# Issuing the row gather of a routed block one block earlier, at the end of the block before

## The chip, the cores and the metric

The kernel runs on one core of a Trainium2 chip. The metric is the device time of one execution in microseconds (us), from several runs; a profile of one more execution shows what each engine did. The engines are PE (TensorE: matmuls and transposes; its weight loads are listed as PEld), DVE (VectorE), ACT (ScalarE), POOL (GpSimd) and SP (SyncE, which here only issues DMAs).

## The reference

Three independent results make the output: a chunked attention, a mixture of four experts over 2304 tokens, and a routed mixture of eight experts, the last of which the change touches. Its core is:

```
expert_idx = np.argmax(logits, axis=1)
gate_w = probs[np.arange(N), expert_idx]
out = np.zeros((N, D), dtype=np.float32)
for e in range(E):
    mask = expert_idx == e
    xe = x[mask]
    h = np.maximum(xe @ w1[e], 0.0)
    ye = h @ w2[e]
    out[mask] = gate_w[mask, None] * ye
```

N is 2304, D 512, the inner size F 1024, E 8. Each token goes through the two weight matrices of one expert only, so the tokens of an expert must be collected (gathered), worked on together, and their results put back (scattered) to where the tokens stand.

## The kernel before, in words

Attention and the first mixture come first. During them the routing of the second mixture is worked out, and a table in DRAM, `slots`, lists which token stands in which slot and with which gate weight. The rows of the tokens lie in DRAM as `ytok`. The last part of the program (from about 785 us to the end at 1102) works through this table in **blocks** of at most 256 slots, one expert to a block.

`step` runs one block as 8 chunks of 128 inner columns. A chunk multiplies the block's rows, transposed (`x`), by a piece of the first weights (ps_h: lines L483 to L485 for a full block, a PAIR; L500 and L501 for a block of 192 rows, a MID), lets ACT and DVE make the activation out of ps_h (L488 and L489, or L506, L507, L511, L514), and later multiplies it by a piece of the second weights (ps_o, L543). Full precision is kept by splitting numbers into a high and a low part (L430 on ACT, L431 on DVE). `single` runs a block of 128 rows in plain fp32 matmuls (L1340 first, L1332 second).

Around the chunks of a block stand:

- `fetch_slots`: SP loads the slots of the block after the next one into `slot_then` (L939).
- `gather_y`: POOL casts the token numbers of the next block to integers (`src`, L942), and issues two indirect DMAs that gather 128 rows of 2 KB each from ytok into yb0 and yb1 (L944).
- `prep`: in the block's last chunk PE transposes the gathered rows (L955, eight transposes for 256 rows), and ACT and DVE write `x` for the next block (L961, L962).
- `finish_parts`: in the first chunk of the block after, ACT scales the results into an `ot` buffer (L983; L975 first adds the parts of a smaller piece), and POOL scatters them to the output by an indirect DMA (L984). The row numbers for it, `dst`, are written by DVE in the fourth chunk (L1353 in `single`, L1422 in `step`), once the scatter that reads the old ones has landed.

The slots move on through three buffers, `slot_then` to `slot_next` to `slot_now`, by two DVE copies in the first chunk of each block (L1394 and L1396).

How many blocks of each kind are needed depends on the routing, so most blocks stand under nested conditions `tc.If(counts > u)` that each engine tests by itself (L1451 for the PAIR blocks, L1462 and L1464 for a MID with a `single` behind it, L1473 and L1475 for further MIDs). In this run these are executed: the blocks 0 to 3 (unconditional), one PAIR, three times a MID and a `single`, one MID, and the last PAIR. Where the rest of a nest is skipped, each engine adds to its semaphores what the skipped blocks would have added; POOL does it for the counters of its DMAs. These places are called joins below. They are at about 939 us (J1, L1451), 1046 us (J2, L1464) and 1067 us (J3, L1475).

Each engine executes its instructions in the order in which this code issues them.

Of the kernel before, what the change touches and what calls it, by code (L numbers as in the profile page):

```python
# [24 lines left out]
KF = FF // P  # L25
# [9 lines left out]
NFIRST = 3  # L35
# [30 lines left out]
def attn_moe_moe2(ctx, tc, att, probs, wg, wgt, w12, m2w, out):  # L66
    nc = tc.nc
# [16 lines left out]
    def ps(tag):  # L84
        return ring(psum, "ps_" + tag, {"h": 2, "o": 4, "m": 2}[tag], [P, 512], F32)
# [51 lines left out]
    slots = dram.tile([NSLOT, 2], F32, name="slots")  # L137
# [173 lines left out]
    def x_sums(which=slice(0, 4)):  # L311

        b11, b21 = xraw[:, 0, 0:2, :], xraw[:, 0, 2:4, :]
        b12, b22 = xraw[:, 1, 0:2, :], xraw[:, 1, 2:4, :]
        t1, t2, t4 = [xsum[:, i] for i in range(3)]
        for out, a, b in ((t1, b12, b11), (t2, b22, t1), (b12, b22, b12), (t4, b21, t2))[which]:
            nc.gpsimd.tensor_tensor(out=out, in0=a, in1=b, op=ALU.subtract)

    def x_split(g):
        raw = (xraw[:, 0, 0:2, :], xsum[:, 0], xsum[:, 1], xraw[:, 1, 2:4, :], xraw[:, 1, 0:2, :],  # L320
               xraw[:, 0, 2:4, :], xsum[:, 2])[len(xs[g])]
        xh, xl = x_slot()
        nc.scalar.copy(xh, raw)
        nc.vector.tensor_tensor(out=xl, in0=raw, in1=xh.bitcast(F32), op=ALU.subtract)
        xs[g].append((xh, xl))
# [120 lines left out]
    def split_lows():  # L446

        while lows:
            lows.pop(0)()
# [248 lines left out]
    buf = {}  # L698
# [237 lines left out]
    def fetch_slots(c, to):  # L936
        assert c in ready or c < NFIRST
        row = nc.sync.value_load(start32[0:1, c:c + 1], min_val=0, max_val=NSLOT - BLK)
        nc.sync.dma_start(out=buf[to], in_=slots[bass.ds(row, BLK), :].rearrange("(i p) c -> p i c", p=P))  # L939

    def gather_y():
        nc.gpsimd.tensor_copy(buf["src"], buf["next"][:, :, 1])  # L942
        for i in range(2):
            nc.gpsimd.indirect_dma_start(  # L944
                out=buf["y"][i], out_offset=None, in_=ytok,
                in_offset=bass.IndirectOffsetOnAxis(ap=buf["src"][:, i:i + 1], axis=0),
                bounds_check=NT - 1, oob_is_err=False,
            )

    def prep(one=False):  # L950

        for i in range(1 if one else 2):
            tp = ps("m")
            for k in range(KD):
                nc.tensor.transpose(tp[:, k * P:(k + 1) * P], buf["y"][i][:, k * P:(k + 1) * P], ident)  # L955
            tpv = tp.rearrange("p (k x) -> p k x", x=P)
            xh, xl = [buf["x"][:, :, q, i * P:(i + 1) * P] for q in range(2)]
            if one:
                nc.scalar.copy(buf["xone"], tpv)
                continue  # L960
            nc.scalar.copy(xh, tpv)  # L961
            nc.vector.tensor_tensor(out=xl, in0=tpv, in1=xh.bitcast(F32), op=ALU.subtract)  # L962
# [92 lines left out]
    for g in range(1, len(GROUPS)):  # L1055
        pcs = att_pieces(g)
        if g == 1:
            then = [x_sums] + [lambda g=g: x_split(g)] * 7
        else:
            then = [lambda k=k: x_sums(slice(k, k + 1)) for k in range(4)] + [lambda g=g: x_split(g)] * 2  # L1060
# [211 lines left out]
    for i in range(NPLAIN):  # L1272
        e, fc = divmod(i, KF)
# [38 lines left out]
    def hold(banks, sizes):  # L1312
        held.append((banks, sizes))
# [5 lines left out]
    def single(s, c):  # L1319

        first = NM1 + s * KF
        assert [stream[q] - first for q in ("load", "split", "freed")] == [KF, 0, 0], (s, stream)
        stream["at"] = s, c
        stream["split"] = first + KF
        stream["limit"] = first + 2 * KF
        x = buf["xone"]
        o = rings["ps_o"][1][2]
        parts = {}

        def second(fc):  # L1330
            raw, h = parts.pop(fc)
            nc.tensor.matmul(o, lhsT=h, rhs=raw[-1][:, -D:], start=(fc == 0), stop=(fc == KF - 1))  # L1332

        for fc in range(KF):
            stream["call"] += 1
            raw, _ = raws.pop(first + fc)
            raw = raw if isinstance(raw, tuple) else (raw,)
            hp = ps("h")
            for k in range(KD):
                nc.tensor.matmul(  # L1340
                    hp[:, :P], lhsT=raw[0][:, k * P:(k + 1) * P], rhs=x[:, k, :], start=(k == 0), stop=(k == KD - 1)
                )
            h = buf["one"][fc]
            nc.scalar.activation(h, hp[:, :P], AF.Relu)
            parts[fc] = (raw, h)
            if fc == 0:
                nc.vector.tensor_copy(buf["now"], buf["next"])
                nc.vector.tensor_copy(buf["next"], buf["then"])
                gather_y()
            for _ in range(2 if 2 * fc < len(buf["raw_one"]) else 0):  # L1350
                load_next()
            if fc == 3:
                nc.vector.tensor_tensor(out=buf["dst"], in0=buf["now"][:, :, 1], in1=over[:, c, :], op=ALU.add)  # L1353
                fetch_slots(c + 2, "then")
            if fc >= LAGONE:
                second(fc - LAGONE)
            if fc == KF - 1:
                prep()
            if fc >= KF - NSPLIT:
                split_next()  # L1360
                split_lows()
        for fc in range(KF - LAGONE, KF):
            second(fc)
        hold([o], ONE)
        stream["freed"] = first + KF
        ahead = [stream[q] - first - KF for q in ("load", "split", "freed")]
        assert ahead == [KF, NSPLIT, 0] and not lows, (s, ahead)

    def step(s, c, sizes, one=False):

        ends = [finish_parts(*h) for h in held]
        held.clear()
        for end in ends:
            next(end, None)
        banks = []
        rings["ps_o"][0] = 0
        x = buf["x"]
        if sizes == PAIR:
            x = (lambda k: buf["x"][:, k, 0]), (lambda k: buf["x"][:, k, 1])
        more = s < NSTEP - 1  # L1380

        second = s == NFIRST - 1
        stream["at"] = s, c
        stream["stop"] = NM1 + (s + 1) * KF if one else NCHUNK
        if s >= NFIRST:
            stream["limit"] = NM1 + (s + 1) * KF
        for fc in range(KF):
            chunk(NM1 + s * KF + fc, x, sizes, fc, banks, True, finish if one else hold,
                  [lambda: prep(one)] if fc == KF - 1 and more else [])
            if fc == 0:  # L1390
                for end in ends:
                    for _ in end:
                        pass
                nc.vector.tensor_copy(buf["now"], buf["next"])  # L1394
                if more and not second:
                    nc.vector.tensor_copy(buf["next"], buf["then"])  # L1396
                    gather_y()
            if s <= NFIRST:
                if s + fc == 0:
                    flush(1)  # L1400
                    sides.append(last_routing())
                else:
                    side()
            if fc == 0 and more:
                ahead = s + 2 < NFIRST or s >= NFIRST
                if s < NFIRST:
                    stream["limit"] = NM1 + (s + (3 if s + 2 < NFIRST else 2)) * KF
                if second:
                    fetch_slots(c + 1, "next")
                elif ahead:  # L1410
                    fetch_slots(c + 2, "then")
            if fc == 0 and s >= NFIRST:
                stream["limit"] = NM1 + min(s + 2, NSTEP) * KF
            if second and fc == 2:
                gather_y()
            if second and fc == 4:
                fetch_slots(c + 2, "then")
            if s == NFIRST and fc == KF // 2:

                split_next()  # L1420
            if fc == 3:
                nc.vector.tensor_tensor(out=buf["dst"], in0=buf["now"][:, :, 1], in1=over[:, c, :], op=ALU.add)  # L1422
        flush()
        split_lows()
        if s == NFIRST:
            side(99)

        if one:
            stream["stop"] = NCHUNK
            while stream["load"] < NM1 + (s + 2) * KF:  # L1430
                load_next()
            assert stream["split"] == NM1 + (s + 1) * KF
        elif NFIRST <= s < NSTEP - 1:
            ahead = [stream[q] - NM1 - (s + 1) * KF for q in ("load", "split", "freed")]
            assert ahead == [KF, NSPLIT, 0] and not (lows or lates or pending), (s, ahead)
# [14 lines left out]
    s = NFIRST + 1  # L1450
# [78 lines left out]
```

## Time and profile before

| | |
|---|---|
| time, median of 3 runs | 1107.29 us (1106.66 to 1107.65) |
| time of the profiled execution | 1104.12 us |
| its span, first to last instruction | 1102.2 us |
| mean granted TensorE clock | 0.996 |
| PE busy | 1073.9 us, 97% |
| DVE busy | 790.7 us, 72% |
| ACT busy | 603.7 us, 55% |
| POOL busy | 252.6 us, 23% |

The span is what the profile's rows cover; the time adds what lies around it. Busy shares are averages over the whole program. The change touches only the last 315 us, and there only a few of the blocks, so the rows below are of stretches of a few microseconds.

### The profile page before, as it was taken

To read this page: it belongs to the slowest core of one execution; us is meant where nothing else is said; L and a number is where in the kernel's file an instruction comes from. 1 tells how busy PE (TensorE), PEld (TensorE's weight loads), DVE (VectorE), ACT (ScalarE), POOL (GpSimd) and SP (SyncE) were. 2 spreads that over 40 slices of the span, in tenths; PEclk is the share of its full clock that TensorE was granted. 3 is DMA by queue.
4 is the path that set the end of the run, shared out by engine and by line. 5 is a ranking of instruction groups with operands and counts; after the bars stand their busy time and mean duration, and the time that the engine had idled before them with its cause. 6 is when DMAs were issued, how large, how long until landed. Compare 5 with 4: busy or idle time off the path is not lost. (4 is left out here: it accounts for less than half of the span.)

```text
span 1102.2 us, 20735 instructions
## 1 busy us (share of the span) xinstructions
PE 1073.9 (97%) x7732; PEld 950.8 (86%) x7733; DVE 790.7 (72%) x1436; ACT 603.7 (55%) x1087; POOL 252.6 (23%) x289
## 2 busy tenths in 40 slices
PE   6999999999999999999999999999999999999895
PEld 5999898888988898988888989898888889877685
DVE  6778887768787877686886678787755966455371
ACT  4555556555656555656555655645455455455461
POOL 1004635556210113220110420111121311212110
PEclk9999999999999999999999999999999999999998
DMA  7878545545554444453434463445627375777850
GB/s 256 284 247 293 190 155 170 167 143 183 189 179 144 134 160 137 155 188 124 153 111 143 121 197 125 139 152 125 250 96 271 126 268 218 278 252 262 303 193 19
DMA packets 83050, 201.10 MB, mean 182 GB/s; under 512 B 13039, under 2 KB 20335, under 8 KB 82801
## 3 DMA queue, kind: packets, MB, share of 16 engines
q1 hardware_dynamic: 74816, 174.90, 47.1%
q0 software_dynamic: 8112, 24.67, 6.2%
q8 instruction: 66, 1.08, 0.4%
q14 instruction: 56, 0.45, 0.2%
HBM read 180.44 MB, written 19.88 MB: 182 GB/s over the span
## 5 line engine op out<-in xcount | busy, mean ns | idle before, releaser
L431 DVE TENSOR_TENSOR wl<-raw,wh 128x1024 fp32r<-128x1024 f32 (+1 forms) x258 | 306.1, 1195 | 35.5 <-ACT wh L430 32.9
L430 ACT CAST wh<-raw 128x1024 fp32r<-128x1024 f32 (+1 forms) x258 | 253.5, 997 | 5.7 <-POOL raw L421 2.5
L1116 PE MATMUL ps_h<-xh,wh 128*128 128x256 f32 x868 | 247.1, 285 | 0.7 <-DVE scr L1168 0.6
L1116 PE MATMUL ps_h<-xl,wh 128*128 128x256 f32 x868 | 244.6, 282 | 0.0
L1116 PE MATMUL ps_h<-xh,wl 128*128 128x256 f32 x868 | 243.9, 281 | 0.0
L1211 PE MATMUL ps_o<-wh,hl 128*128 128x512 f32 x496 | 194.8, 393 | 0.0
L1211 PE MATMUL ps_o<-wh,hh 128*128 128x512 f32 x496 | 194.7, 393 | 0.0
L1211 PE MATMUL ps_o<-wl,hh 128*128 128x512 f32 x496 | 194.1, 391 | 0.0
L1174 POOL TENSOR_TENSOR scr<-scr 128x256 f32<-128x256 f32 x64 | 70.0, 1094 | 459.8 <-ACT scr L1173 402.8
L1116 PEld LDWEIGHTS ps_h<-xh,wh 128*128 128x128 f32 x868 | 163.4, 188 | 11.9 <-DVE scr L1168 1.0
L1116 PEld LDWEIGHTS ps_h<-xl,wh 128*128 128x128 f32 x868 | 163.3, 188 | 8.7
L1116 PEld LDWEIGHTS ps_h<-xh,wl 128*128 128x128 f32 x868 | 164.6, 190 | 0.0
L1186 DVE SCALAR_TENSOR_TENSOR hl<-scr,hh 128x512 fp32r<-128x512 f32 x128 | 94.2, 776 | 72.0 <-ACT hh L1185 72.0
L1211 PEld LDWEIGHTS ps_o<-wh,hl 128*128 128x128 f32 x496 | 93.1, 188 | 21.4 <-DVE hl L1186 0.6
L1190 ACT COPY scr<-ps_h 128x256 f32<-128x256 f32 x64 | 23.9, 374 | 146.5 <-PE ps_h L1116 129.0
L1211 PEld LDWEIGHTS ps_o<-wh,hh 128*128 128x128 f32 x496 | 93.8, 189 | 11.1
L1211 PEld LDWEIGHTS ps_o<-wl,hh 128*128 128x128 f32 x496 | 93.4, 188 | 10.9
L543 PE MATMUL ps_o<-wh,hh 128*128 128x512 f32 x232 | 88.7, 402 | 0.0
L582 DVE CUSTOM_DVE_ANT_0 junk<-y,wgb 128x512 bf16<-128x512 f32 x112 | 84.8, 757 | 2.0
L543 PE MATMUL ps_o<-wl,hh 128*128 128x512 f32 (+1 forms) x204 | 79.4, 392 | 0.0
L488 ACT ACTIVATE hh<-ps_h 128x256 fp32r<-128x256 f32 x80 | 30.7, 384 | 85.5 <-PE ps_h L485 81.9
L1185 ACT ACTIVATE hh<-scr 128x512 fp32r<-128x512 f32 x128 | 74.0, 628 | 3.3 <-DVE scr L1178 3.1
(287 smaller groups left out, 1879.6 us busy)
## 6 DMA issues: line engine op xcount, KB each, us to landing
raw<-in_w SPq DMA_DIRECT2D x96, 512.0 KB, 4.5
raw<-wsum SPq DMA_DIRECT2D x48, 512.0 KB, 3.6
raw<-in_w SPq DMA_DIRECT2D x80, 256.0 KB, 3.6
raw<-in_m2w SPq DMA_DIRECT2D x40, 512.0 KB, 9.7
xraw<-in_m2w SPq DMA_DIRECT2D x20, 512.0 KB, 6.0
wgb<-in_m2w SPq DMA_DIRECT2D x19, 512.0 KB, 8.0
atkq<-in_att SPq DMA_DIRECT2D x17, 512.0 KB, 5.8
wsum<-raw POOLq DMA_DIRECT2D x16, 512.0 KB, 3.0
```

The lines of the kernel that those rows point to most:

```text
L430: nc.scalar.copy(wh[:, c], raw[:, c])
L431: lows.append(lambda: nc.vector.tensor_tensor(out=wl[:, c], in0=raw[:, c], in1=wh[:, c].bitcast(F32), op=ALU.subtract))
L488: nc.scalar.activation(hh, hp[:, :n], AF.Relu)
L543: nc.tensor.matmul(y, lhsT=l, rhs=r, start=(fc == 0 and q == 0), stop=(fc == KF - 1 and q == len(parts) - 1))
L582: nc.vector.tensor_tensor_reduce(out=junk, in0=tiles[i], in1=wgb[:, e, :], scale=1.0, scalar=0.0, op0=ALU.mult, op1=ALU.add, accum_out=lg[ ...
L1116: nc.tensor.matmul(out, lhsT=l[:, c], rhs=r[:, k, :], start=first and k + q == 0, stop=last and k == 1 and q == 2, skip_group_check=True,)
L1174: nc.gpsimd.tensor_tensor(out=s3, in0=s3, in1=s5, op=ALU.add)
L1185: nc.scalar.activation(h[0][:, c], src, AF.Relu)
L1186: nc.vector.scalar_tensor_tensor(out=h[1][:, c], in0=src, scalar=0.0, in1=h[0][:, c].bitcast(F32), op0=ALU.max, op1=ALU.subtract)
L1190: nc.scalar.copy(s2, a)
L1211: nc.tensor.matmul(banks[i], lhsT=l[:, c], rhs=r[:, d], start=q + f + k == 0, stop=q == NPAIRS - 1 and f == 1 and k == 2,)
```

## The change

Before, a block's first chunk issues the gather for the next block, from the slots just moved into `slot_next`. After, the gather is issued at the end of a block, behind the transposes in `prep` which read yb, and it takes the rows of the block after the next one, straight from `slot_then`. Blocks 0 to 2 stay as they were; block 3 does both, which makes the step from the one scheme to the other.

```
-    def gather_y():
-        nc.gpsimd.tensor_copy(buf["src"], buf["next"][:, :, 1])
+    def gather_y(slots="next"):
+        nc.gpsimd.tensor_copy(buf["src"], buf[slots][:, :, 1])
...
@@ single
             if fc == 0:
                 nc.vector.tensor_copy(buf["now"], buf["next"])
                 nc.vector.tensor_copy(buf["next"], buf["then"])
-                gather_y()
...
             if fc == KF - 1:
                 prep()
+                gather_y("then")
...
@@ step
                 if more and not second:
                     nc.vector.tensor_copy(buf["next"], buf["then"])
-                    gather_y()
+                    if s <= NFIRST:
+                        gather_y()
+            if fc == KF - 1 and more and s >= NFIRST:
+                gather_y("then")
```

NFIRST is 3, KF is 8. Line numbers of the functions stay the same up to `prep` and `finish_parts`; the conditions move down by three (L1451 becomes L1454, L1464 becomes L1467, L1475 becomes L1478).

On POOL the first place is the last of the PAIR blocks under L1451 and the instructions with which POOL skips blocks; the block that is executed before J1 stands in the same order. Before:

```order
L1451 COMPARE_AND_BRANCH
L984 DMA out<-ot_8577,dst 2304x512 [waits DMASW0_49,DMASW1_49,DVE_49,Activation_49]
L984 DMA out<-ot_8578,dst 2304x512 [waits Activation_49]
L942 CAST src<-slot_next 128x2 [waits DMASW3_49,DMASW2_49,DVE_49]
L944 DMA yb_6628<-ytok,src 128x512 [waits PE_49,Pool_49]
L944 DMA yb_6629<-ytok,src 128x512 [waits PE_49]
L1451 UNCONDITIONAL_BRANCH
L1451 ISA [waits Pool_49,DMASW6_49,DMASW7_49,DMASW5_49,DMASW4_49]
L1451 UNCONDITIONAL_BRANCH
L1451 ISA [waits Pool_49,DMASW4_49,DMASW5_49,DMASW3_49,DMASW6_49,DMASW2_49,DMASW7_49,DMASW1_49,DMASW0_49]
```

The same place of the changed kernel:

```order
L1454 COMPARE_AND_BRANCH
L984 DMA out<-ot_8577,dst 2304x512 [waits DMASW2_49,DMASW3_49,DVE_49,Activation_49]
L984 DMA out<-ot_8578,dst 2304x512 [waits Activation_49]
L942 CAST src<-slot_then 128x2 [waits DMAHW6_49,DMASW5_49,DMASW4_49]
L944 DMA yb_6628<-ytok,src 128x512 [waits PE_49,Pool_49]
L944 DMA yb_6629<-ytok,src 128x512 [waits PE_49]
L1454 UNCONDITIONAL_BRANCH
L1454 ISA [waits Pool_49,DMASW6_49,DMASW7_49,DMASW1_49,DMASW0_49]
L1454 UNCONDITIONAL_BRANCH
L1454 ISA [waits Pool_49,DMASW4_49,DMASW5_49,DMASW3_49,DMASW6_49,DMASW2_49,DMASW7_49,DMASW1_49,DMASW0_49]
```

DMASW are the counters of POOL's DMAs, DMAHW those of SP's. Within the block the order on POOL is the same, but the cast now waits for the slot fetch of SP (DMAHW) and not for DVE's copy, and the gathers' wait for PE is now for the transposes in the same block's last chunk, not for those of the block before. The ISA rows are the additions for skipped blocks; the second of those shown, like the others behind it, waits for all eight counters.

On POOL the second place is a MID and the `single` behind it, up to the test that decides on the next pair of them. Before:

```order
L984 DMA out<-ot_8577,dst 2304x512 [waits DMASW1_49,DMASW4_49,DMASW0_49,DMASW5_49,DVE_49,Activation_49]
L984 DMA out<-ot_8578,dst 2304x512 [waits Activation_49]
L942 CAST src<-slot_next 128x2 [waits DMASW6_49,DMASW3_49,DMASW7_49,DMASW2_49,DVE_49]
L944 DMA yb_6628<-ytok,src 128x512 [waits PE_49,Pool_49]
L944 DMA yb_6629<-ytok,src 128x512 [waits PE_49]
L984 DMA out<-ot_8578,dst 2304x512 [waits DMASW4_49,DMASW5_49,DVE_49,Activation_49]
L984 DMA out<-ot_8577,dst 2304x512 [waits Activation_49]
L942 CAST src<-slot_next 128x2 [waits DMASW7_49,DMASW6_49,DVE_49]
L944 DMA yb_6628<-ytok,src 128x512 [waits PE_49,Pool_49]
L944 DMA yb_6629<-ytok,src 128x512
L1464 COMPARE_AND_BRANCH
```

The same of the changed kernel:

```order
L984 DMA out<-ot_8577,dst 2304x512 [waits DMASW2_49,DMASW3_49,DMASW1_49,DMASW6_49,DMASW0_49,DMASW7_49,DVE_49,Activation_49]
L984 DMA out<-ot_8578,dst 2304x512 [waits Activation_49]
L942 CAST src<-slot_then 128x2 [waits DMASW4_49,DMASW5_49,DMASW1_49,DMAHW3_49,DMASW0_49,Pool_49]
L944 DMA yb_6628<-ytok,src 128x512 [waits PE_49,Pool_49]
L944 DMA yb_6629<-ytok,src 128x512
L984 DMA out<-ot_8578,dst 2304x512 [waits DMASW6_49,DMASW7_49,DVE_49,Activation_49]
L984 DMA out<-ot_8577,dst 2304x512 [waits Activation_49]
L942 CAST src<-slot_then 128x2 [waits DMAHW0_49,DMASW1_49,DMASW0_49]
L944 DMA yb_6628<-ytok,src 128x512 [waits PE_49,Pool_49]
L944 DMA yb_6629<-ytok,src 128x512
L1467 COMPARE_AND_BRANCH
```

The third and fourth scatters are those of the MID's own results, issued in the `single`. The two gathers ahead of them now belong to the MID's last chunk, and the last two to the last chunk of the `single`, directly ahead of the test.

On ACT the place is the join J1 and the first chunk of the MID behind it. Before:

```order
L1451 UNCONDITIONAL_BRANCH
L1451 UNCONDITIONAL_BRANCH [waits Activation_49] x7
L1462 COMPARE_AND_BRANCH
L983 ACTIVATE ot_8577<-ps_o_168,slot_now 128x512 [waits DMASW0_49,DVE_49,DMASW4_49,PE_49,Activation_49]
L983 ACTIVATE ot_8578<-ps_o_169,slot_now 128x512 [waits DMASW1_49,DMASW5_49,PE_49,Activation_49]
L506 COPY scr<-ps_h_314 128x192 [waits DVE_49,PE_49]
```

The same of the changed kernel:

```order
L1454 UNCONDITIONAL_BRANCH
L1454 UNCONDITIONAL_BRANCH [waits Activation_49] x7
L1465 COMPARE_AND_BRANCH
L983 ACTIVATE ot_8577<-ps_o_168,slot_now 128x512 [waits DMASW0_49,DMASW2_49,DVE_49,DMASW6_49,PE_49,Activation_49]
L983 ACTIVATE ot_8578<-ps_o_169,slot_now 128x512 [waits DMASW3_49,DMASW1_49,DMASW7_49,PE_49,Activation_49]
L506 COPY scr<-ps_h_314 128x192 [waits DVE_49,PE_49]
```

The order on ACT is the same. Its first instructions behind the join wait for counters of POOL's DMAs in both kernels; other counters stand there because the DMAs of a block are dealt to the eight counters in a different turn.

## Rows read from the trace of the kernel before

**Rows 1.** The page: busy time, share of the span and instructions of each engine.

```profile
PE 1073.9 (97%) x7732; PEld 950.8 (86%) x7733; DVE 790.7 (72%) x1436; ACT 603.7 (55%) x1087; POOL 252.6 (23%) x289
```

**Rows 2.** Waits of PE and PEld, 785 to 1102: total us, times, longest us.

```profile
PE ps_m L955 <- DMA yb<-ytok,src: 3.3, 3, 1.9
...
PEld ps_m L955 <- DMA yb<-ytok,src: 6.3, 6, 2.1
```

**Rows 3.** Timeline of PE around prep in the first and second `single`: start, length, what.

```profile
968.71 1.02 PE L1332 MATMUL ps_o<-raw_one,scr 128*128 128x512 f32 x2
...
971.29 1.88 PE L1332 MATMUL ps_o<-raw_one,scr 128*128 128x512 f32 x4
...
1003.31 1.02 PE L1332 MATMUL ps_o<-raw_one,scr 128*128 128x512 f32 x2
...
1006.33 1.88 PE L1332 MATMUL ps_o<-raw_one,scr 128*128 128x512 f32 x4
```

**Rows 4.** Timeline of PE and ACT at J1; idle time before, and releaser, in brackets.

```profile
934.22 1.03 PE L955 MATMUL ps_m<-ident,yb 128*128 128x128 f32 x8
...
939.55 1.27 ACT L983 ACTIVATE ot<-ps_o,slot_now 128x512 f32<-128x512 f32 x2 [2.83 <-PEq L1451]
941.46 0.32 ACT L506 COPY scr<-ps_h 128x192 f32<-128x192 f32 x1 [0.64 <-PE ps_h L501]
...
942.41 0.36 PE L500 MATMUL ps_h<-x,wh 128*128 128x384 f32 x1
```

**Rows 5.** Timeline of DVE and PE at the ends of the first two `single` blocks.

```profile
967.83 0.16 DVE L1353 TENSOR_TENSOR dst<-slot_now,over 128x2 int32<-128x2 f32 x1 [6.68 <-DMA out<-ot,dst]
...
972.48 1.28 DVE L962 TENSOR_TENSOR x<-ps_m,x 128x512 fp32r<-128x512 f32 x2
...
974.33 0.74 PE L500 MATMUL ps_h<-x,wh 128*128 128x384 f32 x1
...
1007.16 1.28 DVE L962 TENSOR_TENSOR x<-ps_m,x 128x512 fp32r<-128x512 f32 x2
...
1009.37 0.74 PE L500 MATMUL ps_h<-x,wh 128*128 128x384 f32 x1
```

**Rows 6.** DMA issues, three stretches (from 846.7, 848, 960): median us to landing.

```profile
yb<-ytok,src POOLq DMA_INDIRECT x1, 3.4
...
yb<-ytok,src POOLq DMA_INDIRECT x1, 5.4
...
out<-ot,dst POOLq DMA_INDIRECT x2, 6.3
```

**Rows 7.** POOL's additions at J1 and J3: ns (min/median/max), first and last start.

```profile
L1451 POOLq INC_SWDGE_SEM  x1: 1632/1632/1632, 929.3 to 929.3; - x1
...
L1475 POOLq INC_SWDGE_SEM  x1: 2097/2097/2097, 1058.3 to 1058.3; - x1
```

**Rows 8.** Timeline of POOL in the PAIR block: the two gathers.

```profile
919.72 1.05 POOL L944 DMA_INDIRECT yb<-ytok,src  x1 [0.62 <-POOL src L942]
921.08 1.02 POOL L944 DMA_INDIRECT yb<-ytok,src  x1 [0.30 <-issue]
```

**Rows 9.** DMA issues from 1031.5 to 1032: us to landing of a slot fetch.

```profile
slot_then<-slots SPq DMA_DIRECT2D x1, 2.0 KB, 11.6
```

**Rows 10.** Timeline of ACT and PE at J2.

```profile
1046.16 0.69 ACT L983 ACTIVATE ot<-ps_o,slot_now 128x512 f32<-128x512 f32 x1 [2.05 <-PEq L1464]
...
1049.24 0.36 PE L500 MATMUL ps_h<-x,wh 128*128 128x384 f32 x1
```

**Rows 11.** Timeline of PE and ACT at J3.

```profile
1061.93 1.03 PE L955 MATMUL ps_m<-ident,yb 128*128 128x128 f32 x8
...
1067.60 0.58 ACT L975 COPY ot<-ps_o 64x512 f32<-64x512 f32 x1 [2.63 <-PEq L1475]
...
1070.09 0.38 ACT L488 ACTIVATE hh<-ps_h 128x256 fp32r<-128x256 f32 x1 [0.35 <-PE ps_h L485]
```

**Rows 12.** Windows view, 1094 to 1095: us, busy by engine, granted clock, DMA share, GB/s.

```profile
1094.00:1095.00 1.00, 0.00 (x0) 0.00 (x0) 0.00 (x0) 0.00 (x0) 0.00 (x0) 0.60 0.27 102
```

More of the change, by code (lines that the diff above doesn't have):

```diff
@@ L939, in fetch_slots, with gather_y @@
         nc.sync.dma_start(out=buf[to], in_=slots[bass.ds(row, BLK), :].rearrange("(i p) c -> p i c", p=P))
-    def gather_y():
-        nc.gpsimd.tensor_copy(buf["src"], buf["next"][:, :, 1])
+    def gather_y(slots="next"):
+        nc.gpsimd.tensor_copy(buf["src"], buf[slots][:, :, 1])
         for i in range(2):
@@ L1348, in single @@
                 nc.vector.tensor_copy(buf["next"], buf["then"])
-                gather_y()
             for _ in range(2 if 2 * fc < len(buf["raw_one"]) else 0):
@@ L1358, in single @@
                 prep()
+                gather_y("then")
             if fc >= KF - NSPLIT:
@@ L1396, in step @@
                     nc.vector.tensor_copy(buf["next"], buf["then"])
-                    gather_y()
+                    if s <= NFIRST:
+                        gather_y()
+            if fc == KF - 1 and more and s >= NFIRST:
+                gather_y("then")
             if s <= NFIRST:
```

## The prediction

> **What bounds the kernel now.** I read the page's engine shares first: PE is busy for 97% of the span [rows 1]. Nothing that frees another engine helps unless PE waits for it, and a new wait of PE is a loss to the full. So I next took the chain of waits of PE and of its weight loads over the last phase (785 to 1102), and looked for rows that name the gather: there are two, 3.3 us in three waits and 6.3 us in six, all at L955, prep's transposes [rows 2]. The two overlap, so they are not to be added. The timeline puts all of them into the three executions of `single`; the blocks run by `step` never wait there. Then I read, engine by engine, the three places where guarded blocks that are not run are skipped: the joins. They are J1 at 939 (behind the one pair block that is run, L1451), J2 at 1046 (behind the third `single`, L1464) and J3 at 1067 (behind the one MID block, L1475). There PE, ACT and POOL meet, and there the moved gather ends up.
>
> **What the change can give back.** In the first `single` the matmuls ahead of and behind the transposes start 2.58 us apart, in the second 3.02 [rows 3]. Unhindered it is some 0.87 for the pair of L1332 and 0.8 for the eight transposes, whose undisturbed run takes 1.03 from first start to last end [rows 4] and overlaps what follows: 1.7. So PE loses 0.9 and 1.3. In the third the longest of the three waits of PE, 1.9, stands before the second four [rows 2]. With the gather issued a block earlier these waits go.
>
> What PE gains it must be able to use. Its next block (L500) needs x, whose last part DVE writes (L962). DVE's row writes dst at 967.83 after waiting 6.68 us for the scatter that still reads the old dst, and runs without a gap from there to the end of L962 at 972.48 + 1.28 = 973.76 [rows 5]. PE starts the block at 974.33 now. So the first `single` gives 974.33 - 973.76 = 0.57, about 0.6, not 0.9; the second 1009.37 - (1007.16 + 1.28) = 0.93, about 0.9, not 1.3 [rows 5]. The dst wait is not touched by the change: two gathers now stand ahead of the scatter in POOL's queue, not behind it. They are issued a few us before, so I take the scatter's landing (6.3 us there [rows 6]) as it is. Bounds: landing sooner lets the two gain 0.9 + 1.3 = 2.2; landing later by 1 us eats both, 0. I take -1.5. The third `single` ends in J2 and is booked there.
>
> **What it costs: the joins.** When POOL skips the blocks that are not run, it executes one instruction (L1451, L1464, L1475, "ISA" in the order) that adds the skipped DMAs to the DMA counters, and it waits first for all eight counters of POOL's DMAs, so for all that it has in flight. It takes 1.63 and 2.10 us in two of the joins [rows 7]. Before, the last gather was issued in the block's first chunk and had landed long ago: POOL began its add at 929.3 and 1058.3 [rows 7], some ten us ahead of what stands behind the joins. After, a cast and two gathers stand right before it, issued when the transposes have read yb, and the last must land first.
>
> ACT waits for these counters: the first instruction behind the join, L983 or L975, reads them because the ot buffer that it writes must have been scattered; in the built program the count that it waits for holds the skipped DMAs. Behind it in ACT's queue stand the copies and activations of the new block (L506, L488), behind them DVE's L507 and L489, and for these PE waits in its third chunk, which needs the ps_h of the first. PE itself runs two chunks without them.
>
> The price of a gather: the second is issued 1.36 us after the first [rows 8], the landing is 3.4 us from issue when little else moves and 5.4 for one that follows directly [rows 6]. Near a join I take 3.4, since in the last microseconds of a block the next weights have mostly come; 5.4 is the bound.
>
> - J1: transposes 934.22 to 935.25, first gather about 934.9, second 936.3, landed 939.7, add done 941.3. ACT's L983 stood at 939.55 [rows 4]: 1.8 late. L506 behind it had 0.64 us of slack before [rows 4], so DVE and PE's third chunk, at 942.41 [rows 4], come some **1.2** later.
> - J2: src must first be cast from slot_then, whose fetch took 11.6 us from an issue at 1031.7 [rows 9], so to 1043.3. The cast is then the first thing, the first gather 0.6 later, the second at 1045.3, landed 1048.7, add done 1050.7. L983 (at 1046.16 before, 0.69 us long [rows 10]), L506 (0.32 [rows 4]) and an L507 of about that length put PE's third chunk at about 1052.1; it started at 1049.24 [rows 10]. That is 2.9 late. Two gathers that ran beside the fetch before now run earlier, so the fetch may land up to 1 us sooner; I take half: **2.4**. This is against the time before, so the third `single`'s gain is already swallowed.
> - J3: transposes 1061.93 to 1062.96, second gather 1064.0, landed 1067.4, add done 1069.5. L975 stood at 1067.60: about 2.0 late; L488 had 0.35 of slack [rows 11], and I allow some 0.4 more on the way to PE's third chunk: **1.2**.
>
> With 5.4 for the landings each join costs 2 more (3.2, 4.4, 3.2). If ACT found the count already there, they cost nothing. The remaining edits cost nothing: SP's slot fetch now also waits for POOL's cast, a whole block ahead of its use; DVE's copy of the slots waits for POOL no more; one gather more is issued (14 pairs for 13), whose rows nobody reads, but it is one of those that J3 waits for.
>
> The Trainium skill's page "DMA: Bandwidth & Descriptors", section "Anatomy of one DMA — SWDGE (gpsimd) path", fits 2.0 us plus the bytes over 436e3 per us to such a DMA. As an estimate from it, 256 KB take 2.6 us; the trace has 3.4 at the least [rows 6]. By the page each join would cost 0.8 less and the sum would be +0.9; I keep the row.
>
> **Sum.** -0.6 - 0.9 + 1.2 + 2.4 + 1.2 = **+3.3 us**. The profiled execution took 1104.12 (a span of 1102.2 and 1.92 around it); it would take 1107.4. The median of the runs is 3.17 above the profiled one, so 1107.29 + 3.3 = **1110.6**. A difference under 0.2%, 2.2 us, can't be told from none here.
>
> **Rivals.**
> (a) The joins cost nothing and the waits in `single` go: -0.6 - 0.9 - 1.9 = -3.4, 1103.9. It would take landings of 1.6 us at J1 (939.55 - 1.63 - 936.3) and 1.5 at J3, under half of the lowest row, or a wait of ACT that the add does not gate. For it speaks that all the gather waits really go. 0.13.
> (b) The gathers land sooner than 3.4 or the add waits for less, so that each join costs some 0.5 to 1 less: +0.3 to +1.8, about 1108.3, no difference. 0.25.
> (c) The forecast, 1108.9 to 1112.0. 0.40.
> (d) PE's clock falls at J2. At the end of the program, where PE has nothing left to do, the granted clock is 0.60 of the full one in 1094 to 1095 [rows 12], on its way from 2.4 to 1.2 GHz. PE would idle twice for nearly 3 us around two chunks at J2. At the lower level each us of matmuls takes two; how long it would last no row of this phase shows. I choose four us at half speed, so 2 lost, with 0 and 4 as its ends: 1112.6. 0.12.
> (e) The gathers land in 5.4, +6 at the joins: up to 1116.6, with a middle of 1114. 0.10.
>
> So: faster 0.13; same 0.27 (case b and a little of c); slower 0.60. The range takes half of (a) out at the low end and half of (e) at the high end: 1105.0 to 1114.5.
>
> **What the profile after would show.** The L955 rows waiting for yb are gone, and the two starts at L1332 around them stand 1.7 apart. The dst wait of DVE (some 6.7 us in each `single`) stays. At L1454, L1467 and L1478 POOL's add starts 3 to 5 us behind the last transposes, and ACT's first L983 or L975 behind each join follows its end; PE shows a wait at the third chunk of the next block (ps_h, from DVE), 1 to 3 us, which was not there. I am wrong if ACT starts there before POOL's add is done, if the landings are under 2 us, or if dst moves with the gathers.

## The result, and the profile after

The changed kernel takes 1116.42 us (median of 7 runs, 1113.44 to 1122.26) where the kernel before takes 1107.65 (7 runs, 1106.66 to 1109.46). The ratio is 1.0088, 95% interval 1.0072 to 1.0105: 9.7 us slower by the ratio, 8.8 by the medians. Forecast were 1110.6, 3.3 us more, and a range up to 1114.5, so the sign is right and the size is not: the loss is nearly three times the forecast, and outside the range. The runs also lie further apart than before, 8.8 us against 2.8. One run of all that are reported here, in experiment 8, took 1176.94 us at a mean granted clock of 0.85 and is left out of the comparisons.

The profiled execution took 1114.66 with a span of 1112.2, 10.0 us more than before. First the chain of waits of PE from 785 us on, in the columns of [rows 2]:

```profile
PE ps_h L500 <- DVE scr L507: 5.6, 2, 3.6
PE ps_h L483 <- DVE hl L489: 4.3, 1, 4.3
```

PE's row at L955 is gone, as forecast; PEld keeps one wait of 0.4 us there. In place of PE's row stand three waits in the third chunk behind the joins, 9.9 us in all: 3.58 behind J1, 2.03 behind J2, 4.30 behind J3. None of them was there before.

Where each microsecond went can be counted by blocks. The starts of a block's first matmul, and the last matmul of the program, give these lengths:

| block | before | after | difference |
|---|---|---|---|
| MID behind J1 | 18.91 | 24.32 | +5.41 |
| first `single` | 15.36 | 14.75 | -0.61 |
| MID | 19.24 | 18.99 | -0.25 |
| second `single` | 15.80 | 15.46 | -0.34 |
| MID | 19.24 | 18.91 | -0.33 |
| third `single` and J2 | 18.28 | 16.11 | -2.17 |
| MID behind J2, and J3 | 21.47 | 23.35 | +1.88 |
| last PAIR behind J3 | 22.31 | 28.55 | +6.24 |

The sum is +9.8. The singles and what lies between them give 3.7 back, and the joins take 13.5.

J1 in the timeline of POOL, ACT, DVE and PE (start, length, what, idle time before and its releaser) answers to [rows 4, 8]:

```profile
935.62 1.71 POOL L944 DMA_INDIRECT yb<-ytok,src  x1 [14.23 <-PE ps_m L955]
937.63 1.99 POOL L944 DMA_INDIRECT yb<-ytok,src  x1 [0.30 <-issue]
...
944.24 1.27 ACT L983 ACTIVATE ot<-ps_o,slot_now 128x512 f32<-128x512 f32 x2 [7.52 <-DMA out<-ot,dst]
...
945.75 0.36 DVE L507 TENSOR_TENSOR scr<-ps_h,scr 128x192 f32<-128x192 f32 x1 [7.02 <-ACT scr L506]
...
946.16 0.44 PE L500 MATMUL ps_h<-x,wh 128*128 128x384 f32 x1 [3.58 <-DVE scr L507]
```

POOL's additions at J1 and J3 (ns, first and last start) answer to [rows 7]:

```profile
L1454 POOLq INC_SWDGE_SEM  x1: 1671/1671/1671, 942.5 to 942.5; - x1
...
L1478 POOLq INC_SWDGE_SEM  x1: 2137/2137/2137, 1074.5 to 1074.5; - x1
```

The reader is to see a staircase. POOL issues the second gather at 937.63 and can start its addition only at 942.5; the addition ends at 944.2, and ACT starts at 944.24 (before, at 939.55 [rows 4]); DVE and PE follow. The profile names a scatter as what released ACT: that scatter was long done, it is its counter that the addition sets. The landings of the two gathers (DMA issues at 935.6 and at 937.6, median us from issue to landing) answer to [rows 6]:

```profile
yb<-ytok,src POOLq DMA_INDIRECT x1, 4.6
...
yb<-ytok,src POOLq DMA_INDIRECT x1, 4.8
```

In the timeline J3 (the first three rows) has the same steps. J2 (the last three) has a shorter wait:

```profile
1069.50 1.99 POOL L944 DMA_INDIRECT yb<-ytok,src  x1 [0.30 <-issue]
...
1076.76 0.58 ACT L975 COPY ot<-ps_o 64x512 f32<-64x512 f32 x1 [8.17 <-DMA yb<-ytok,src]
...
1079.60 0.43 PE L483 MATMUL ps_h<-x,wh 128*128 128x256 f32 x1 [4.30 <-DVE hl L489]
...
1044.58 0.41 POOL L942 CAST src<-slot_then 128x2 int32<-128x2 f32 x1 [8.65 <-SPq L1467]
...
1051.80 0.69 ACT L983 ACTIVATE ot<-ps_o,slot_now 128x512 f32<-128x512 f32 x1 [6.04 <-DMA yb<-ytok,src]
...
1053.15 0.44 PE L500 MATMUL ps_h<-x,wh 128*128 128x384 f32 x1 [2.03 <-DVE scr L507]
```

J2 differs in one step. These are POOL's addition there, and the landing of the second gather, which is issued at 1047.31:

```profile
L1467 POOLq INC_SWDGE_SEM  x1: 2087/2087/2087, 1049.6 to 1049.6; - x1
...
yb<-ytok,src POOLq DMA_INDIRECT x1, 4.3
```

The first gather was issued at 1045.40 and landed 4.1 us later, at 1049.5, just ahead of the addition. The second lands at 1051.6, 2.0 us after the addition has begun. So at J2 the addition waits for the first of the two gathers only. In the built program the addition that runs there waits for seven of the eight counters, and the eighth is that of the last gather; those that run at J1 and J3 wait for all eight.

The waits do not account for all of it: J1 costs 5.41 for a wait of 3.58, J3 6.24 for one of 4.30. The windows view (us, busy time of PE, PEld, DVE, ACT and POOL, granted clock, DMA share, GB/s) shows the rest:

```profile
946.00:947.00 1.00, 0.84 (x5) 0.84 (x6) 0.55 (x4) 1.00 (x3) 0.69 (x2) 0.84 0.02 8
947.00:948.00 1.00, 1.00 (x6) 1.00 (x5) 1.00 (x4) 1.00 (x2) 0.89 (x1) 0.50 0.79 263
948.00:949.00 1.00, 1.00 (x5) 0.81 (x4) 1.00 (x3) 0.81 (x4) 0.05 (x1) 0.50 0.45 139
...
1053.00:1054.00 1.00, 0.85 (x5) 0.86 (x6) 0.44 (x4) 1.00 (x3) 0.87 (x1) 1.00 0.02 8
...
1080.00:1081.00 1.00, 1.00 (x7) 1.00 (x6) 0.67 (x2) 1.00 (x3) 0.60 (x1) 0.50 0.61 229
```

The granted clock falls to 0.50 (1.2 GHz) just after PE has started again, behind J1 and behind J3, and stays there for 3.4 us by this view; behind J2, after an idle time of 2.03, it stays at 1.00. Half the clock for 3.4 us can lose 1.7 us, which is most of the remaining 1.8 and 1.9. Experiment 9 tests it.

### The profile page after: what moved, and what is told of

It reads as the page before. It is cut to its first block, busy times and chain, and to the rows that moved or that the text cites. A ratio compares the mean times of both kernels' runs of the same rounds, so it can differ in the third digit from the quotient of the medians.

```text
span 1112.2 us, 20754 instructions
## 1 busy us (share of the span) xinstructions
PE 1077.6 (97%) x7733; PEld 953.9 (86%) x7733; DVE 790.9 (71%) x1436; ACT 602.9 (54%) x1087; POOL 267.1 (24%) x292
```

## The experiments

Two theories stood against each other. **A**: POOL's addition at a join waits for the gathers issued right ahead of it, and all else follows from this lateness. **B**: the moved gathers cost in themselves, by their place in POOL's queue or by contention with the weight loads. The kernel before was run beside each group of kernels, with a median of 1106.8, 1106.1 and 1106.4.

**1. Results behind the joins in buffers of their own.**

```
+        rings["oj"] = [0, [buf["raw_whole"][:, i * D:(i + 1) * D] for i in range(2)]]
...
-            ot = ring(m2, "ot", 2, [P, D], F32)[:n]
+            ot = ring(m2, "oj" if own else "ot", 2, [P, D], F32)[:n]
...
-            finish(*held.pop(0))
+            finish(*held.pop(0), True)
...
-        step(s + 2 * u, CBOTH + 2 * u, MID, one=True)
+        step(s + 2 * u, CBOTH + 2 * u, MID, one=True, own=u == 0)
```

> All gathers stay where the change put them; only the results that ACT scales right behind the three joins go to two buffers of their own (the halves of raw_whole, idle there), whose last scatter lies ahead of the skipped blocks. Theory A (ACT's first write behind a join waits, through its ot buffer, for POOL's addition, and that for the last gather to land): ACT goes on at once, PE's waits of 3.6, 2.0 and 4.3 us in the third chunk go, the clock stays at 1.00, and only the gains are left: 1107.65 - 3.7 = about 1104. Theory B (the moved gathers and their traffic themselves cost the time: queue order on POOL, contention with the weight loads): the gathers are where they were, so about 1116.

Measured: 1112.16 us (1109.81 to 1119.32), ratio 1.0051 (1.0031 to 1.0071). Neither expectation holds: about two fifths of the loss are gone. The chain of waits of DVE and PE says why (the profiled execution is one of 1119.32, the slowest of its six):

```profile
DVE dst L1426 <- DMA out<-raw_whole,dst: 14.2, 2, 7.8
...
PE ps_o L543 <- DVE hh L514: 10.2, 2, 5.8
```

ACT and PE's third chunk go on at once. But POOL's scatters stand behind its addition and are late as well, and DVE's write of dst in the fourth chunk waits for them, with everything queued behind it. The wait has moved by one reader; the lateness is the same.

**2. The early gather only where no join can follow**, at the end of a MID that has a `single` behind it.

```
             if fc == KF - 1:            # single
                 prep()
-                gather_y("then")
...
-                    if s <= NFIRST:
-                        gather_y()
-            if fc == KF - 1 and more and s >= NFIRST:
+                    gather_y()
+            if fc == KF - 1 and one:
                 gather_y("then")
```

> The early gather only at the end of a MID that a single follows, where no skip can stand behind it; a single issues none, and all other blocks gather in their first chunk as before. Theory A: no gather is in flight at a join, so the joins cost what they cost before, and the singles give back 0.6, 0.3 and 2.2 us: about 1104.5. Theory B: the early gathers stand ahead of the MID's scatters and beside the weight loads still, so the singles should lose what they gain, 1107 to 1109.

Measured: 1102.97 us (1099.62 to 1105.12), ratio 0.9964 (0.9952 to 0.9977): faster than the kernel before. The first and third `single` last 14.73 and 16.06 us, as in the changed kernel, the block behind J1 18.91 and the clock is 1.00 there. As A has it. What B says of gathers beside the weight loads and ahead of the MID's scatters does not happen.

**3. The other half**: the early gather at the ends of all other blocks, and the old one in the first chunk of a `single`.

```
                 nc.vector.tensor_copy(buf["next"], buf["then"])
+                gather_y()                     # single, first chunk
...
-            if fc == KF - 1 and more and s >= NFIRST:
+            if fc == KF - 1 and more and s >= NFIRST and not one:
```

> The other half: the early gather at the end of all blocks from the fourth on except a MID that a single follows; a single gathers in its first chunk and again at its end. The gains in the singles are gone, the gathers ahead of the joins stay. Theory A: all of the loss, and none of the gain: 1116.4 + 3 = about 1119, with waits of PE in the third chunk behind each join. Theory B: about half of the loss, some 1112.

Measured: 1117.10 us (1113.93 to 1119.66), ratio 1.0088 (1.0067 to 1.0108). The whole loss is here, as A has it, but the time is not A's 1119. The 3 us of gain that I expected to be missing are largely not missing: the waits for the gather in the singles are 1.5 us there, against 3.3 [rows 2]. So not only the lead of a gather counts there; I did not look further. In this run the clock falls behind J2 too (0.50 from 1057 to 1059 in the windows view), although PE had waited only 1.79 us there.

**4. Extra matmuls in place of the idle time**, read from yb.

```
+            if busy and fc == 2:
+                tp = ps("m")
+                for _ in range(8):
+                    nc.tensor.matmul(tp, lhsT=ident, rhs=buf["y"][0], start=True, stop=True)
```

> The changed kernel, and eight extra fp32 matmuls of 128x512 into a spare PSUM bank (3.4 us at full clock, nobody reads them) ahead of the third chunk of the three blocks behind the joins, so that PE works while it would wait. If the fall of the clock (0.50 for 3 to 4 us behind J1 and J3) comes from PE's idle time there, it goes and the time falls by some 3.4 us to 1113, and the spread of the runs shrinks; PE's remaining wait is what ACT's lateness costs alone, about 10 us less the 10 us of matmuls that hide in it. If the clock falls for another reason, the time stays at about 1116.

Measured: 1128.07 us (1124.57 to 1130.58), ratio 1.0193 (1.0169 to 1.0216). This tells nothing of the clock: the extra matmuls read yb, so they waited for the very gather (4.0 us of waits at this line), and they took 23.0 us, not 10.

**5. Own buffers and a late dst**: experiment 1, and dst written in the seventh chunk, for `step` and `single`.

```
-            if fc == 3:
+            if fc == 6:
                 nc.vector.tensor_tensor(out=buf["dst"], in0=buf["now"][:, :, 1], in1=over[:, c, :], op=ALU.add)
```

> The changed kernel with the two buffers of its own behind the joins (as in the first experiment) and the write of dst in a block's seventh chunk, not its fourth. In the first experiment ACT no longer waited, but the scatters behind POOL's addition were late, and DVE's dst write in the fourth chunk waited 7.8 us for them. Theory A (one lateness of POOL, which only moves to the next wait that reads it): with both readers moved away PE's waits behind the joins shrink to under 2 us in all and the time goes to 1104 to 1106. Theory B (the moved gathers cost in themselves): it stays at about 1112.

Measured: 1100.93 us (1099.61 to 1102.99), ratio 0.9955 (0.9937 to 0.9974). All gathers stand where the change put them, and the kernel is 15 us faster than the changed one and 5 faster than before. POOL's addition at J1, and the timeline of ACT there:

```profile
L1456 POOLq INC_SWDGE_SEM  x1: 1671/1671/1671, 944.4 to 944.4; - x1
```

```profile
941.08 1.26 ACT L984 ACTIVATE raw_whole<-ps_o,slot_now 128x512 f32<-128x512 f32 x2 [2.79 <-PEq L1456]
```

POOL's addition is as late as ever, now behind ACT's start. PE's chain of waits has no row of a third chunk any more, and the block lasts 19.13 us. Theory B is refuted by this run: the same gathers, at the same places, cost nothing that can be told (1100.93 us; experiment 6, which has none of them at a join, 1101.24) once no reader stands close behind the join. Theory A holds with an addition: two readers had to be moved, the write of ot and the write of dst.

**6. Experiment 2 with the late dst.**

> The early gather only at the end of a MID that a single follows (as in the second experiment), and dst written in the seventh chunk. Theory A: with the gather there in time, what still bounds the ends of the singles is DVE, which stands 6 to 7 us at dst and then has all its splits to do; with dst later this wait goes and the singles give back the rest of what the gather cost them, up to 1 us each: 1100 to 1102, against 1103.0. If DVE is not what bounds them there, 1103.

Measured: 1101.24 us (1099.36 to 1103.82), ratio 0.9952 (0.9936 to 0.9968), as expected. The first two singles last 14.51 us each (14.73 and 15.49 with dst in the fourth chunk): DVE was what bounded them. The intervals of the ratios of 2 and 6 overlap, so it is these lengths and not the times that tell the two apart. In the profiled execution the clock fell behind J3, where PE had stood for 1.99 us at the join itself, and the last PAIR lasts 23.69 us and not 22.17 as in experiment 2 (clock 0.50 from 1066 to 1068 in the windows view).

**7. Extra matmuls again**, now ident by ident into a spare bank, 28, 14 and 32 of 128x128.

> The fourth experiment again with extra matmuls that read and write nothing which another engine uses (ident by ident into a spare PSUM bank, 28, 14 and 32 of 128x128, some 3.4, 1.7 and 4 us at full clock, ahead of the third chunk behind the three joins); there the operand was yb, so that PE waited for the gather itself and the next gather for PE. If the clock falls because PE idles behind the joins, the clock is 1.00 throughout and the time some 3 to 4 us under the changed kernel's 1116: 1112 to 1113. If the fall has another cause, about 1116.

Measured: 1117.80 us (1116.49 to 1122.42), ratio 1.0114 (1.0091 to 1.0136). The clock stays at 1.00 behind the joins, but the extra matmuls took 6.43, 3.31 and 7.31 us there, twice what I had counted, more than the waits that they were to fill. PE's waits in the third chunks are gone.

**8. The kernel before with the late dst alone.**

> The kernel before, with dst written in the seventh chunk and nothing else changed. It says what the place of dst is worth by itself. The singles wait for the gather there, so I expect little: DVE's 20 us of waiting go, PE gains at most 1 us in each single: 1105 to 1107.

Measured: 1107.38 us (11 runs, 1104.59 to 1112.51), ratio 1.0014 (0.9997 to 1.0031): no difference that can be told. The waits for the gather in the singles are then 4.4 us. So in the singles the late dst is worth something only where the gather is early, and the early gather its full worth only with the late dst.

**9. Extra matmuls of the right length**, 15, 8 and 17.

> The last experiment with extra matmuls showed the clock at 1.00 throughout, but its extra matmuls took 6.4, 3.3 and 7.3 us (each fp32 matmul is two passes, which I had counted as one), more than the waits they were to fill. Here they are 15, 8 and 17, some 3.4, 1.8 and 3.9 us. Theory A (the clock falls because PE idles behind the joins): the clock stays at 1.00 and the block behind J1 lasts 22.5 us and not 24.3, the one behind J3 about 2 us less too: 1112 to 1113 where the changed kernel has 1116. If the idle time is not the cause: the clock falls all the same, and about 1116.

Measured: 1112.49 us (1111.66 to 1114.46), ratio 1.0064 (1.0049 to 1.0078). At J1, in the timeline, and one us of the windows view:

```profile
941.99 3.53 PE L1391 MATMUL ps_m<-ident 128*128 128x128 f32 x30
946.20 0.45 PE L500 MATMUL ps_h<-x,wh 128*128 128x384 f32 x1 [0.68 <-DVE scr L507]
```

```profile
947.00:948.00 1.00, 1.00 (x8) 0.91 (x7) 1.00 (x4) 1.00 (x3) 0.92 (x1) 1.00 0.77 263
```

The third chunk starts 6.56 us into its block, 0.47 later than in the changed kernel (6.09), but the clock behind it is 1.00 and not 0.50, as behind the other two joins, and the ratio falls from 1.0088 to 1.0064, by 2.7 us (the two intervals overlap a little). So the fall of the clock comes from PE's idle time. The block behind J1 lasts 23.21 us, not the 22.5 expected; 0.47 of that is the later third chunk. In the changed kernel the time goes with the clock: its mean is 0.994 in the fastest run and 0.989 in the two slowest. Here it is 0.995 to 0.997, and the runs lie within 2.8 us. But the clock is not the whole of the spread: in experiment 7 it is 0.995 or 0.996 in every run, and the runs lie 5.9 us apart.

**10. The changed kernel with the late dst alone**, the fourth corner beside 1 and 5.

> The changed kernel with dst written in the seventh chunk and the ot buffers as they are: the fourth corner of the square (as changed; own ot behind the joins; late dst; both). Theory A: ACT's write into ot behind the joins still waits for POOL's addition, so PE's waits in the third chunk stay at about 10 us and the clock falls there; only the singles gain, up to 1.5 us: about 1114. If the late dst was what mattered in the corner with both: about 1101.

Measured: 1120.46 us (1116.85 to 1123.28), ratio 1.0134 (1.0117 to 1.0151): not 1114, and slower than the changed kernel. The ot readers wait as before, as A has it. The first two singles do last 14.51 us. But at J2 PE waits 2.94 us, not 2.03: the third `single` is only 0.14 us shorter, but the slot fetch that the gather there needs took 10.8 us, not 9.9. Now the clock falls at J2 too:

```profile
1052.00:1053.00 1.00, 0.00 (x0) 0.00 (x0) 0.40 (x2) 1.00 (x3) 0.00 (x0) 0.86 0.00 0
1053.00:1054.00 1.00, 0.99 (x3) 0.99 (x4) 0.44 (x3) 1.00 (x4) 1.00 (x1) 0.50 0.06 16
```

The MID behind J2 is 2.3 us longer than in the changed kernel, the last PAIR 1.4, and that is more than the three `single` blocks gain, 1.3. Whether the late dst makes the slot fetch slower is not shown; the profile is of one execution.

## Why the prediction was wrong in size

**The gains** were sized rightly at the first `single`: -0.6 forecast, -0.61 measured, and for the reason given, DVE behind its dst wait. The first starts around its transposes are now 1.7 us apart:

```profile
974.13 1.02 PE L1332 MATMUL ps_o<-raw_one,scr 128*128 128x512 f32 x2
...
975.87 1.88 PE L1332 MATMUL ps_o<-raw_one,scr 128*128 128x512 f32 x4
...
973.06 0.16 DVE L1352 TENSOR_TENSOR dst<-slot_now,over 128x2 int32<-128x2 f32 x1 [6.77 <-DMA out<-ot,dst]
```

At the second it was -0.34 and not -0.9. There DVE's dst wait grew from 6.80 to 7.47 us, one of the bounds I had set (a later landing of the scatter), and PE now waits 0.37 for x. That the third `single` reaches J2 2.2 us earlier, as I had booked it inside J2's term, is right.

**The mechanism of the loss** was right at each step at J1 and J3: POOL's addition waits for the gathers, ACT's first write behind the join for the addition, DVE for ACT, and PE in its third chunk for DVE. Experiments 1, 2, 3 and 5 show it. At J2 one step was wrong: I let the addition wait for all that POOL has in flight, and there it did not wait for the last gather.

**The step that failed is the price of the joins**, +1.2, +2.4 and +1.2, which is the sum's whole loss. At J1 and J3 it was mis-sized in three of its parts, and one was left out:

- *The start.* I let the first gather be issued when half of the transposes were done, at 934.9. POOL's wait did end there, but the issue starts only at 935.62: 0.7 us that I had left out.
- *The issue.* I took the distance of the two gathers from a block in which they take 1.05 and 1.02 us [rows 8]. Here the first takes 1.71: 0.65 more until the second.
- *The landing.* I chose 3.4 us, the lower of two rows [rows 6], and kept 5.4 as a rival with a chance of 0.10, although 5.4 is the row of a gather that follows another directly, as the one that the addition waits for does. It was 4.8 at J1 and 4.9 at J3: 1.4 more. The Trainium skill's fit ("DMA: Bandwidth & Descriptors", "Anatomy of one DMA — SWDGE (gpsimd) path") gives 2.6 by estimate, further off still; the trace does not agree with it.

Together they make 2.8 us: the addition at J1 ends at 944.2 and not at 941.3, and the third chunk starts 3.75 us late and not 1.2. At J3 the same parts make 3.0 us: the second gather is issued 3.58 us behind the first transpose and not 2.07, and lands 1.5 later; PE waits 4.30.

- *The clock.* I had it only as a rival (0.12), and only at J2, because I took PE's idle time at J1 and J3 to be short. It fell at J1 and J3 and cost most of 1.8 and 1.9 us; with the right lateness both idle times are longer than those at J2.

At J2 I was too high: the slot fetch took 9.9 us (issued at 1034.52) and not 11.6, and was issued 1.1 us sooner in its `single`, so that PE waited only 2.03. Two further errors cancel there, which is luck: the second gather was issued 2.9 us behind the fetch's landing and not 2.0, and landed in 4.3 and not 3.4, but the addition did not wait for it. It starts 5.2 us behind the fetch's landing, where I had 5.4. Against the time before, the `single` and J2 and the MID behind it together give 0.3 back; I had them at +2.4.

So the sum with the terms as they were measured is -0.6 - 0.3 - 0.6 (the two MIDs) + 5.4 - 0.3 + 6.2 = +9.8, where it stood at +3.3. The range was too narrow because it treated the landing and the clock as separate, unlikely cases. They belong together: a later landing makes a longer idle time, and in the last phase of these runs each of the nine that lasted 2.9 us or more came with a fall of the clock (experiments 1, 3 and 10 and the changed kernel).

## What to carry to other kernels

Ahead of a place where an engine must wait for its DMAs (here a skipped branch; no other kind was tried), a transfer issued early is no longer free: its whole landing lies on the path of whoever reads that engine's counters next. Issue it early only where no such place follows, or move the readers away from it; removing one reader moves the wait to the next one, so list them all. And price a stall of TensorE with the clock that it may lose behind it: here that made up to 3.4 of 13.5 us.

The version to keep is that of experiment 6: the gather ahead only in the MID blocks that feed a `single`, and dst late. It takes 1101.2 us, 5 less than before; experiment 5 is not to be told from it.

## What the runs showed of the hardware

- The granted clock fell with idle times of PE of 3.58 and 4.30 us (changed kernel), of 3.71, 2.94 and 4.85 us (experiment 10), and also of 1.79 us (experiment 3, J2) and 1.99 us (experiment 6, J3). It did not fall with 2.03 us (changed kernel, J2) or 2.57 us (experiment 8, third `single`), nor where extra matmuls left less than 1 us ahead of the third chunks (experiment 9). So these runs give no length that divides the two. It fell between 1.2 us before PE worked again (experiment 10, J3) and 1.3 us after (experiment 6) and came back within some 4 us, once within 7 (experiment 10, J3).
- Issuing an indirect gather takes POOL 1.00 to 1.06 us at some places and 1.7 to 2.0 at others. In the changed kernel the quick ones (961.92, 995.62) stand where the DMA engines' busy share is 1.03, and their rows land in 6.4 to 6.9 us; the slow ones (935.62, 976.98, 1067.28) stand where it is 0.19 to 0.35 and land in 4.1 to 4.9. But one pair at a share of 0.20 took only 1.39 and 1.01, and in experiment 8 two gathers took 1.89 (998.49, 1033.74) where the share is 1.02 and 1.03. What makes an issue slow stays open; no run tested it.
- The addition for skipped blocks takes POOL 1.63 to 2.14 us. At J1 and J3 of the changed kernel it starts when the last gather has landed, at J2 when the first of the last two has.
